# First v products from raw fp32 weights, a last product that accumulates in place, and a new order

## The chip, the cores and the metric

The kernel runs on one core of a Trainium2 chip. Its time is the device time of that core in microseconds (us). It is one program with five instruction queues: TensorE (PE in the rows), VectorE (DVE), ScalarE (ACT), GpSimd (POOL) and SyncE (SP), which only starts DMA transfers. Each queue runs in its own order, and the queues wait for each other by semaphores. The runs of the kernel before have a median of 493.95 us (492.88 to 494.36).

## The reference

One layer norm feeds two branches, and their product is added to the input:

```python
def _A_ref(x, wqkv, w_phi, wo):              # S = 2048 tokens, D = 512, H = 32 heads of 16
    q, k, v = (x @ wqkv) per head
    pq, pk  = q @ w_phi, k @ w_phi           # per head, 16 x 16
    phi_q   = concat(softmax(pq), softmax(-pq));  phi_k likewise
    kv, z   = phi_k^T v, sum over tokens of phi_k
    o       = (phi_q kv) / (phi_q z + 1e-6)
    return o @ wo
def _B_ref(x, w1, b1, w2):                   # F = 1792
    return mish(x @ w1 + b1) @ w2
xn  = layernorm(x)
out = x + _A_ref(xn, ...) * silu(_B_ref(xn, ...))
```

Everything is in fp32.

## The kernel before

**Number format.** Most matmuls take the fast fp32r format. An operand is split into a high part (a copy into fp32r on ScalarE) and a low part (source minus high part, on VectorE or GpSimd), by `split`, and a product of two split operands is three matmuls: low x high, high x low, high x high (`blocks`, `mm3`). Transposes, the folds of `w_phi` into the q and k weights, the kv sums and the numerators are plain fp32 matmuls.

**Seven products for eight.** The 2048 tokens are handled as 16 tiles of 128, two tiles to a chunk c. A chunk times a 512-row weight is computed as seven half-size products on sums and differences of the blocks. `norm(t)` normalizes and transposes tile t into the PSUM tile `pt`. For an even tile it splits the transposed blocks; for an odd tile it also forms the four differences `xs` and splits those (`fh`, `fl` hold the parts). For k and v these products are `kv_a` to `kv_d` (tiles `kx`, `ky`, `kz`). Chunk 0 is an exception: `FRONT = 1` sends it through `direct(c, i)` (tile `kj`), which takes the plain blocks, so that it needs no differences of the weights. i = 0, 1 give v of tiles 0 and 1, i = 2, 3 give k. Each `kj` is 12 matmuls of 128x512, since each of its four blocks takes three.

**Stages.** First the k weights are folded (`wkf`), then k and v of all chunks with the softmax features and their sums (`kvp`), mixed with the first FFN product of tokens 0 to 1023 (`fx`, `fy`, `fz`, parts Fa0 to Fd6). Then q (`qx`, `qy`, `qz`), the denominators (`den`), and the first FFN product of tokens 1024 to 2047 (Fa7 to Fd13). For these the split w1 blocks are loaded again from DRAM, tiles `w1b`, parts M0 to M6 (`again1`). Then numerators (`pn`), the output projection (`pw`), and the second FFN product (`y`, parts G), of which the last eighth of the tokens (T = 7) is done product by product over all seven weight blocks. `final` adds up its products, applies silu, multiplies and stores.

**What sets the order.** The code only records operations. `ORDER` lists the parts; TensorE runs its work in just that order. `Program.simulate` then places the other engines' operations around it: each has a due time (the TensorE time of what needs it, less its own duration, shifted by an entry of `SHIFT`), an operation recorded by `either` or `copy` may go to one of two engines, and tiles come from pools with a fixed number of buffers (38 of `slot`, 15 of `s2`, 8 PSUM banks). A tile is taken when its first operation is placed, and its buffer waits for the tile that held it before. What comes out is a fixed instruction list for each queue.

**Names in the rows.** Every operation is issued from one line, L397 before and L403 after. `wv0h`, `wv0l`, `wv1h`, `wv1l` are the parts of the raw v weights `wvr`; `wkh`, `wkl` those of the folded k weights; `ws1` to `ws4` the weight sums and differences. `xh`, `xl` (x12_) are the first half of tile 1. `xc` are the blocks of chunks 4 to 7. `hd` is the FFN's hidden layer in DRAM, `r` a block of it read back.

Of the kernel before, what the change touches and what calls it, by code (L numbers as in the profile page):

```python
# [39 lines left out]
A0 Kd2 Fa0 Ka4 Kb3 Fb0 Fc0 N10 Kc3 A1 Kb4 N11 Kd3 Fd0 A2 N14 N12 P4 Kc4 Ka5 Kd4 N13 Kb5 Kc5 Kd5 Fa4 Ka7 Fb4 Fc4 Ka6  # L40
N15 Fd4 Kb6 A3 P6 Kc6 Kb7 Kd6 Kc7 P2 A4 P3 A5 Fa6 Fa3 Fb6 Fa2 P1 Fb3 Fc6 Fc3 Kd7 P5 wQ Fa1 Fb2 Fd3 Fd6 M4 Fc2 A6 A7
Fa5 Fb1 Q0 Fb5 Fc1 z Fd1 Fc5 D0 D1 Q1 M3 Q2 D2 L D3 Q3 Fd5 Fa11 Fd2 Fa10 M5 Fa12 Fb10 Fb11 D4 Fc11 D5 Fc10 M6 Q4 Fd11
D8 D6 Q7 Fa13 wo0 D7 M1 Fb12 Fc12 Q5 D9 M0 Fd12 Fb13 wo1 D10 Fc13 Fa8 Fd10 D11 Q6 Fd13 Ub0 M2 Fb8 Fc8 Fd8 Fa9 Fa7 Fb7
Fb9 Ua0 Fc9 Fc7 O0 R0 D12 O5 D13 O7 O6 O1 D14 D15 Fd7 R2 O2 Ub1 Fd9 O3 R6 O4 Ua1 R1 G7 R3 G8 O9 O15 R4 O10 G9 O13 O11
G10 G11 O8 R5 O14 O12 G12 G13 G21 G35 G36 G37 E1 G38 H1 G22 G39 G40 G41 G23 G24 E5 G0 G25 G26 G27 G1 G2 G3 G28 E3 G29
H5 G30 G31 G32 G4 G5 G6 G33 G34 E4 E0 G42 G43 H4 G14 G15 G44 G45 G46 G16 G17 H3 H0 G18 G19 G47 G48 G20 E6 G49 E7 E2 H6
H2
# [2 lines left out]
N0:2:-4600 N0:5:5000 kh:3:-4800 N4:2:1800 N4:6:-2800 N1:15:300 N1:23:-3700 N1:24:4800 wq0:2:1600 wq0:4:900 N3:17:15000  # L50
ks:1:-500 ks:2:-4900 N5:14:-600 Kd0:7:-800 N7:10:-2000 N7:11:2000 N7:16:5800 Kb1:1:-5100 N8:1:5000 N8:11:2000
N9:5:3000 N9:6:-800 N9:7:-800 Kc1:2:3600 Fa0:3:7000 N10:1:300 N11:0:-5000 Kd2:3:-3000 Kd2:4:15000 Kd2:7:300 Kd3:3:2000
Ka5:3:5800 Kd4:3:-200 Kd4:9:2000 N15:13:-3600 Kd5:3:-2000 P6:1:-800 P6:10:1600 Fc4:4:-4200 P5:3:800 Kc6:9:-1100
Kc7:2:-800 Kc7:7:10000 Kc7:9:4700 Kd6:1:800 Kd6:3:-1700 A4:0:5800 Kd7:7:6800 Fc3:5:5000 Fa5:1:300 Fc2:1:-3000
wQ:2:-800 wQ:6:-5000 Q0:15:2000 Fc5:2:-5800 P1:12:-300 Fa1:4:-3200 Q2:13:1700 Q2:20:-600 Fb1:3:-2000 D3:0:1100
D3:1:300 Fc1:2:-7300 Q4:14:-3000 D5:6:1900 M5:3:2000 D6:4:-2500 D6:8:2300 M2:0:300 D8:10:-2000 D7:6:500 Q6:5:3900
Q6:16:8000 Q5:5:1700 Q5:20:-2000 Q5:25:5300 Fb12:3:800 D9:7:1300 Fd12:1:4200 Fd12:2:-5000 D11:6:4800 Ub0:4:-300
Ub0:12:-2800 Ub0:13:-1500 Fc9:2:5300 D13:0:7100 D13:1:-3400 D13:2:300 M1:2:11200 Q7:3:-6200 Q7:20:-4300 Q7:22:5000
Q7:23:-1300 Q7:25:4200 Fb7:1:1600 Ua0:11:5000 Ua0:14:2000 D14:1:700 D14:5:-5900 D14:7:600 Fc7:2:8300 D15:9:-2000
D15:10:-1300 R0:1:-1600 R0:5:800 Ub1:2:-2700 Ub1:12:10200 Fd8:1:1100 R2:7:-5000 R3:1:800 R1:7:5600 R5:4:300 R5:6:-5300  # L60
G10:1:5000 G11:2:800 R6:1:-5000 E1:0:-15000 O15:2:800 E4:0:-1300 E4:3:5000 G36:0:2000 G37:1:3800 G39:4:2500 G0:1:3200
G0:6:1200 G3:3:-5000 G3:5:12900 G22:0:2000 G5:6:1400 G23:6:700 G24:3:300 G27:1:300 H0:0:10000 G43:2:-3800 H5:3:2600
G14:5:-5000 G15:1:2000 G16:4:4800 G46:3:-2600 G47:6:-4100 H3:5:-5000 E2:2:-4700 E2:3:1300 G49:6:4200 G49:16:-1600
# [1154 lines left out]
```

## Time and profile before

| | |
|---|---|
| median of 3 runs | 493.95 us (492.88 to 494.36) |
| profiled execution | 493.94 us, of which the span of the core is 492.2 us |
| TensorE busy | 481.9 us, 98% of the span |
| VectorE busy | 455.8 us, 93% |
| ScalarE, GpSimd busy | 292.7 us (59%), 253.8 us (52%) |
| HBM | 60.60 MB read, 44.43 MB written |

The span is the profiler's time from the first to the last instruction of the core; 1.74 us of the execution lie outside it. In a row of the timeline the first number is the start, the second how long the group lasted, x8 that eight instructions were merged, and the bracket how long the engine had been idle and what ended that. PE rows are matmuls and PEld rows their weight loads, which overlap. One plain fp32 matmul is recorded as two instructions.

### The profile page before, as it was taken

What the parts mean: (1) busy time and instruction counts of PE and PEld (TensorE: products, weight loads), DVE (VectorE), ACT (ScalarE), POOL (GpSimd) and SP (SyncE); (2) the same over time, 40 slices, a digit from 0 to 9 for tenths busy, and PEclk for the clock granted to TensorE, in tenths of its full rate; (3) what the DMA queues carried; (4) which work ended last, traced back from release to release, by engine and by line L of the source; (5) the groups of instructions that cost most, each with busy time, mean ns of one, the idle gap of its engine ahead of it and who ended that gap; (6) DMA issues with size and microseconds to landing.
All of it is one profiled execution on the core that took longest, in us unless ns stands there. A gap on an engine that the chain in (4) does not pass through costs nothing.

```text
span 492.2 us, 10298 instructions
## 1 busy us (share of the span) xinstructions
PE 481.9 (98%) x3808; PEld 426.2 (87%) x3808; DVE 455.8 (93%) x897; ACT 292.7 (59%) x450; POOL 253.8 (52%) x196
## 2 busy tenths in 40 slices
PE   6999999999999999999999999999999999999996
PEld 6987878888888989889887778788899999999996
DVE  6999999999998889998999889989989999989984
ACT  2978556555555453633444535576778688598631
POOL 2689989988726356785757775470050302030010
PEclk8999999999999999999999999999999999999999
...
GB/s 291 226 107 55 200 237 83 281 159 294 317 368 366 306 207 243 388 367 249 118 157 326 233 90 298 99 225 192 173 193 164 202 192 161 207 192 278 153 136 56
DMA packets 68642, 105.70 MB, mean 215 GB/s; under 512 B 6896, under 2 KB 37744, under 8 KB 68592
## 3 DMA queue, kind: packets, MB, share of 16 engines
...
q10 hardware_dynamic: 144, 0.26, 0.1%
...
HBM read 60.60 MB, written 44.43 MB: 213 GB/s over the span
## 4 chain that ended last, share of the span: by engine, by line
PE 93%; DMA 4%; DVE 2%; SPq 1%; issue 0%; ACT 0%
PE y L397 29%; PE fx L397 15%; PE pw L397 9%; PE kx L397 8%; PE fy L397 8%; PE qx L397 4%; PE ky L397 4%; PE fz L397 3%; DMA w1b<-w1d 3%; PE kj L397 2%; PE qy L397 2%; PE kz L397 2%; PE pt L397 2%; PE pn L397 2%; PE kvp L397 2%; DMA wkT<-wqkT 1%
## 5 line engine op out<-in xcount | busy, mean ns | idle before, releaser
L397 ACT ACTIVATE ah<-r 128x896 fp32r<-128x896 f32 x56 | 51.2, 944 | 16.0 <-DVE r L397 11.0
L397 DVE TENSOR_TENSOR al<-r,ah 128x896 fp32r<-128x896 f32 x50 | 54.6, 1123 | 1.2 <-ACT ah L397 0.9
L397 POOL TENSOR_TENSOR r<-r 128x128 f32<-128x128 f32 (+1 forms) x18 | 9.2, 525 | 85.5 <-DVE r L397 35.1
L397 DVE TENSOR_TENSOR r<-r 128x128 f32<-128x128 f32 (+1 forms) x150 | 48.0, 367 | 2.6 <-ACT r L397 1.8
L397 PE MATMUL y<-w2h,al 128*128 128x256 f32 x160 | 45.4, 284 | 0.0
L397 PE MATMUL y<-w2l,ah 128*128 128x256 f32 x160 | 45.3, 283 | 0.0
L397 PE MATMUL y<-w2h,ah 128*128 128x256 f32 x160 | 45.3, 283 | 0.0
L397 PE MATMUL y<-w2t,ah 128*128 128x256 f32 x224 | 40.8, 283 | 0.0
L397 PE MATMUL fx<-fh,w1b 128*128 128x512 f32 x112 | 39.2, 394 | 0.9 <-DMA w1b<-w1d 0.9
L397 ACT ACTIVATE r<-r 128x512 f32<-128x512 f32 x56 | 33.4, 621 | 6.7 <-DMA r<-hd 6.7
L397 PEld LDWEIGHTS y<-w2t,ah 128*128 128x128 f32 x224 | 34.9, 192 | 0.0
L397 PE MATMUL y<-w2t,al 128*128 128x256 f32 x112 | 31.7, 283 | 0.0
L397 PEld LDWEIGHTS y<-w2h,al 128*128 128x128 f32 x160 | 30.7, 192 | 0.5 <-issue 0.4
L397 PEld LDWEIGHTS y<-w2l,ah 128*128 128x128 f32 x160 | 30.7, 192 | 0.1
L397 PEld LDWEIGHTS y<-w2h,ah 128*128 128x128 f32 x160 | 30.7, 192 | 0.0
L397 PE MATMUL y<-w2g,ah 128*128 128x256 f32 x160 | 30.4, 283 | 0.0
L397 PEld LDWEIGHTS fx<-fh,w1b 128*128 128x128 f32 x112 | 21.0, 188 | 6.7 <-DMA w1b<-w1d 1.7
L397 PEld LDWEIGHTS y<-w2g,ah 128*128 128x128 f32 x160 | 24.9, 192 | 0.0
L397 PE MATMUL fx<-fl,w1b 128*128 128x512 f32 x56 | 22.0, 392 | 0.9 <-DMA w1b<-w1d 0.9
L397 PE MATMUL y<-w2g,al 128*128 128x256 f32 x80 | 22.6, 283 | 0.0
L397 POOL TENSOR_TENSOR xx<-sr,xx 128x512 f32<-128x512 f32 x2 | 2.6, 1292 | 38.4 <-DVE xx L397 38.4
L397 PEld LDWEIGHTS y<-w2t,al 128*128 128x128 f32 x112 | 21.5, 192 | 0.0
...
## 6 DMA issues: line engine op xcount, KB each, us to landing
...
```

Of the source, the lines that this page charges most:

```text
L397: ins = getattr(e, m)(*a, **k)
```

## The change

1. For tiles 0 and 1, `norm` first copies the transposed tile from PSUM to an SBUF tile `xf` (`flat[t]`). All that read `pt` of these tiles read `xf` then. With the source in SBUF, GpSimd may do their low parts and differences as well (`tt = either`), and the copy `xr` of the first half is dropped for chunk 0.
2. v of tiles 0 and 1 (`direct`, i < 2) is computed as four plain fp32 matmuls of `xf` with the raw weights `wvr`, in place of twelve fp32r matmuls on split parts.
3. The masked copy `phit` of `w_phi` may run on GpSimd too.
4. In the last eighth of the FFN, the bank of product 2 is first filled with a copy of product 1, and product 2 accumulates on it. `final` then applies silu right out of PSUM and has no addition there.
5. `ORDER` and `SHIFT` are new tables, and one constant of the planner's transfer times changed.

```diff
 ORDER = """
-wv0 kh N0 N2 N6 kd N1 wv1 kl ks Ka0 wq1 b1 N3 wq0 Kd0 Kb0 N7 Ka1 Kc0 k2 k4 N4 N5 Kb1 N8 Kc1 Ka2 Ka3 N9 P0 Kb2 Kd1 Kc2
+wv0 N0 b1 N1 kh kl N2 N3 Kc0 wv1 Ka1 Kb0 kd N4 N6 ks wq0 N5 Kd0 Ka0 N7 Ka2 k2 wq1 Kb1 P0 k4 Kc1 Ka3 N8 N9 Kb2 Ka4 Kd1
...
@@ simulate
-                dma = max(dma, now + (1100 if now > 2500 else 1350) + (READ if reads(calls[0][1]) else WRITE))
+                dma = max(dma, now + (1100 if now > 2500 else 1750) + (READ if reads(calls[0][1]) else WRITE))
@@ block_kernel
-    V.tensor_tensor(phit.rearrange("p g (j b) -> p g j b", b=DH), phic[:, :, None, :].to_broadcast([P, KC, 8, DH]),
+    either(phit.rearrange("p g (j b) -> p g j b", b=DH), phic[:, :, None, :].to_broadcast([P, KC, 8, DH]),
@@ norm
+        if t < 2 * FRONT:
+            flat[t] = s2(f"xf{t}").rearrange("p (k n) -> p k n", k=KC)
+            copy(flat[t], pt)
+            pt = flat[t]
         c, p0 = t // 2, pts.get(t // 2)
+        tt = either if c < FRONT else V.tensor_tensor
...
-                    split(pt[:, 2 * x:2 * x + 2], *xc[c][x])
+                    split(pt[:, 2 * x:2 * x + 2], *xc[c][x], tt)
...
-        split(pt[:, 2:4], *xc[c][2])
-        x12 = alloc("s2", [P, 2, P], f"xr{c}")
+        split(pt[:, 2:4], *xc[c][2], tt)
...
-            split(pt[:, 0:2], *x12_[c])
-        copy(x12, pt[:, 0:2])
+            split(pt[:, 0:2], *x12_[c], tt)
+            x12 = pt[:, 0:2]
+        else:
+            x12 = alloc("s2", [P, 2, P], f"xr{c}")
+            copy(x12, pt[:, 0:2])
...
-            V.tensor_tensor(d[:, i], a, b, op=ALU.subtract)
+            tt(d[:, i], a, b, op=ALU.subtract)
@@ direct
-        lhs = [xc[c][0], xc[c][1]] if t % 2 == 0 else [x12_[c], xc[c][2]]
-        for j, (a, (h, l)) in enumerate(zip(((0, 1), ("k", 2))[i // 2], lhs)):
-            blocks(ps, lambda k: (h[:, k], l[:, k]), lambda k: tuple(t[:, k] for t in wkv[a]), j == 0, j == 1)
         if i < 2:
+            for j in range(2):
+                with one():
+                    for k in range(2):
+                        PE.matmul(ps, flat[t][:, 2 * j + k], wraw["v", j][:, k], start=j == k == 0, stop=j == k == 1)
             vs[t] = s2(f"v{t}")
...
+        lhs = [xc[c][0], xc[c][1]] if t % 2 == 0 else [x12_[c], xc[c][2]]
+        for j, (a, (h, l)) in enumerate(zip(("k", 2), lhs)):
+            blocks(ps, lambda k: (h[:, k], l[:, k]), lambda k: tuple(t[:, k] for t in wkv[a]), j == 0, j == 1)
@@ ffn2
-                            PE.matmul(ps, lhs[u], v, start=k not in opened, stop=b == NB - 1 and u == 0 and v is wh, skip_group_check=True)
+                            PE.matmul(ps, lhs[u], v, start=k not in opened and (n, last) != (2, True),
+                                      stop=b == NB - 1 and u == 0 and v is wh, skip_group_check=True)
...
+            if last and n == 2:
+                copy(at(2)[0], at(1)[0])
@@ final
-            if n == 8 and not DIRECT:
+            if n == 8:
                 u = base
-            else:
+            elif n != 2:
                 plus_(u, base, y(n))
-            A.activation(u, u, AF.Silu)
+            A.activation(u, y(2) if n == 2 else u, AF.Silu)
```

**What stands where: the start, on TensorE.** Before, behind the nine warm-up matmuls (wkf and wqf are folds, four matmuls each):

```order
L397 MATMUL wkf01_147<-phit_101,wkT00_137 128x128 x4
L397 MATMUL wkf11_148<-phit_101,wkT01_138 128x128 x4
L397 MATMUL pt0_154<-ident_83,x0_151 128x128 x4
L397 MATMUL pt2_162<-ident_83,x2_157 128x128 x4
L397 MATMUL pt6_170<-ident_83,x6_165 128x128 x4
L397 MATMUL pt1_178<-ident_83,x1_175 128x128 x4
L397 MATMUL wkf21_189<-phit_101,wkT10_139 128x128 x4
L397 MATMUL wkf31_190<-phit_101,wkT11_140 128x128 x4
L397 MATMUL kj00_194<-wv0h_142,fl00_104 128x512
```

In the change, at the same place:

```order
L403 MATMUL pt0_149<-ident_83,x0_146 128x128 x4
L403 MATMUL pt1_156<-ident_83,x1_153 128x128 x4
L403 MATMUL wkf01_164<-phit_101,wkT00_137 128x128 x4
L403 MATMUL wkf11_165<-phit_101,wkT01_138 128x128 x4
L403 MATMUL wkf21_169<-phit_101,wkT10_139 128x128 x4
L403 MATMUL wkf31_170<-phit_101,wkT11_140 128x128 x4
L403 MATMUL pt2_178<-ident_83,x2_173 128x128 x4
L403 MATMUL pt3_180<-ident_83,x3_175 128x128 x4
L403 MATMUL kj03_183<-wkh0_161,xl0_160 128x512
```

The transposes of tiles 0 and 1 now come first, and the first `kj` is k of tile 1, where it was v of tile 0. Behind the 12 matmuls of `kj03` and the products `kx1`, `kz1` of chunk 1 follow:

```order
L403 MATMUL kz1_193<-wv1h_190,fh10_105 128x512
L403 MATMUL kj01_195<-wvr0_141,xf1_157 128x512 x2
L403 MATMUL kj01_195<-wvr1_189,xf1_157 128x512 x2
L403 MATMUL pt4_206<-ident_83,x4_201 128x128 x4
L403 MATMUL pt6_214<-ident_83,x6_209 128x128 x4
L403 MATMUL wqf01_220<-phit_101,wqT00_218 128x128 x4
L403 MATMUL wqf11_221<-phit_101,wqT00_218 128x128 x4
L403 MATMUL pt5_223<-ident_83,x5_203 128x128 x4
```

The four `kj01` matmuls are the new fp32 ones.

**On ScalarE, at the same place** (from its first work on a matmul's result). Before:

```order
L397 ACTIVATE wkh0_144<-wkf01_147 128x512
L397 ACTIVATE x2_157<-x2_157,nb2_161,rs2_155 128x512
L397 ACTIVATE wv0h_142<-wvr0_141 128x1024
L397 ACTIVATE fh00_103<-pt0_154 128x2x128
L397 ACTIVATE wkh0_144<-wkf11_148 128x512
L397 ACTIVATE wv1h_184<-wvr1_183 128x1024
L397 ACTIVATE fh20_107<-pt1_178 128x2x128
L397 ACTIVATE fh00_103<-pt2_162 128x2x128
```

In the change:

```order
L403 ACTIVATE xf0_150<-pt0_149 128x512
L403 ACTIVATE fh00_103<-xf0_150 128x2x128
L403 ACTIVATE fh10_105<-xf0_150 128x2x128
L403 ACTIVATE xf1_157<-pt1_156 128x512
L403 ACTIVATE xh0_159<-xf1_157 128x256
L403 ACTIVATE fh20_107<-xf1_157 128x2x128
L403 ACTIVATE fh30_109<-xs0_158 128x2x128
L403 ACTIVATE wkh0_161<-wkf01_164 128x512
L403 ACTIVATE wv0h_142<-wvr0_141 128x1024
L403 ACTIVATE wkh0_161<-wkf11_165 128x512
L403 ACTIVATE fh40_111<-xs0_158 128x2x128
L403 ACTIVATE wkh1_166<-wkf21_169 128x512
```

Before, the high part of the first fold (`wkh0`) stood first; now seven activations on tiles 0 and 1 stand ahead of it. The next two after these rows are `wv1h` and the last `wkh1`.

**On SP, at the last loads of w1 for the first FFN product** (tiles w1b; hd are stores of the hidden layer). Before:

```order
L397 DMA w1b12_800<-w1d21_450 128x768 [waits DMAHW1_49,PE_49]
L397 DMA w1b02_799<-w1d20_449 128x768 [waits DMAHW2_49,PE_49]
L397 DMA hd36_768<-hb13_758 128x512 [waits DMAHW3_49]
L397 DMA hd26_719<-hd13_790 128x512 [waits DMAHW4_49,Activation_49]
L397 DMA hd31_806<-hc8_805 128x512 [waits DMAHW5_49,DVE_49]
L397 DMA w1b22_801<-w1d22_451 128x1024 [waits DMAHW6_49,Pool_49]
L397 DMA hd21_772<-hd8_807 128x512 [waits DMAHW7_49,Activation_49]
L397 DMA hd31_806<-hb8_804 128x512 [waits DMAHW0_49,DVE_49]
L397 DMA w1b32_802<-w1d23_452 128x1024 [waits DMAHW1_49,PE_49]
```

In the change:

```order
L403 DMA w1b12_781<-w1d21_382 128x768 [waits DMAHW3_49,PE_49]
L403 DMA w1b30_774<-w1d03_259 128x1024 [waits DMAHW4_49,PE_49]
L403 DMA hd23_656<-hd10_761 128x512 [waits DMAHW5_49,Activation_49]
L403 DMA hd35_760<-hb12_742 128x512 [waits DMAHW6_49,DVE_49]
L403 DMA w1b02_780<-w1d20_381 128x768 [waits DMAHW7_49,PE_49]
L403 DMA hd21_769<-ha8_768 128x512 [waits DMAHW0_49,DVE_49]
L403 DMA hd25_717<-hd12_770 128x512 [waits DMAHW1_49,DVE_49]
L403 DMA w1b22_782<-w1d22_383 128x1024 [waits DMAHW2_49,PE_49]
L403 DMA w1b32_783<-w1d23_384 128x1024 [waits DMAHW3_49,PE_49]
```

Which instruction each waits for stands in the program's wait counts. Before, the load of `w1b32` (the last block, fx9) waits for the second matmul of `fx7` on `fl01`, and 19 matmuls of 128x512 stand between that one and the first that uses `w1b32`; a little earlier, the load of `w1b21` (fx8) waits for a GpSimd scaling of tile 7's q features (`q7e`), which follows VectorE's denominators. In the change, between the matmul that each of the four loads of the last block waits for and its first use stand 120 to 148 matmuls; among the last sixteen loads the fewest behind such a wait are 54 (`w1b31`). Four of these sixteen wait for others: `w1b05`, `w1b11` and `w1b21` for GpSimd, `w1b25` for VectorE.

**The end, on VectorE.** Before:

```order
L397 TENSOR_TENSOR xx15_1_1182<-u15_1_1184,xx15_1_1182 128x256
L397 TENSOR_TENSOR u15_0_1187<-yc0_1171,y74_1170 128x256
L397 TENSOR_TENSOR u15_0_1187<-u15_0_1187,sr15_0_1186 128x256
L397 TENSOR_TENSOR xx15_0_1185<-u15_0_1187,xx15_0_1185 128x256
L1214 UNCONDITIONAL_BRANCH
```

In the change:

```order
L403 TENSOR_TENSOR u15_1_1195<-u15_1_1195,sr15_1_1194 128x256
L403 TENSOR_TENSOR xx15_1_1193<-u15_1_1195,xx15_1_1193 128x256
L403 TENSOR_TENSOR u15_0_1198<-u15_0_1198,sr15_0_1197 128x256
L403 TENSOR_TENSOR xx15_0_1196<-u15_0_1198,xx15_0_1196 128x256
L1234 UNCONDITIONAL_BRANCH
```

The addition of product 2 (`y74`) to product 1 is gone from the end of the queue. ScalarE's copy `y74<-y70` needs product 1 alone, and five products of 21 matmuls (6, 5, 7, 4 and 3) run on TensorE between product 1 and product 2.

More of the change, by code (lines that the diff above doesn't have):

```diff
@@ L38 @@
 ORDER = """
-wv0 kh N0 N2 N6 kd N1 wv1 kl ks Ka0 wq1 b1 N3 wq0 Kd0 Kb0 N7 Ka1 Kc0 k2 k4 N4 N5 Kb1 N8 Kc1 Ka2 Ka3 N9 P0 Kb2 Kd1 Kc2
[L40 to L47, printed above, removed]
+wv0 N0 b1 N1 kh kl N2 N3 Kc0 wv1 Ka1 Kb0 kd N4 N6 ks wq0 N5 Kd0 Ka0 N7 Ka2 k2 wq1 Kb1 P0 k4 Kc1 Ka3 N8 N9 Kb2 Ka4 Kd1
+Kc2 Kb3 A0 Fa0 Kc3 Kd2 Fb0 Fc0 P4 N10 A1 N11 Kd3 Fd0 Kb4 Kc4 N12 Fa4 Fb4 Kd4 P2 A2 Ka5 N13 Fc4 Fd4 N14 Kb5 Kc5 Ka6 N15
@@ new lines @@
+Kd5 Kb6 A3 A4 Fa2 Ka7 P6 Kc6 P3 Kb7 Kc7 Fb2 Kd6 Fa3 Fc2 Kd7 Fb3 Fa6 Fc3 Fb6 Fc6 P1 wQ Fa1 Fd6 Fb1 A5 A6 Fd3 A7 Fd2 M3
+P5 Q0 Fa5 Fc1 z Fb5 D0 Fc5 Q1 D1 Fd1 Q3 L D2 D3 Fd5 M4 Q2 M6 D4 Fa10 D5 Fb10 Fa11 Fb11 Fc10 Q4 Fc11 D6 Fa13 Fb13 Fc13
+Fd13 Q6 M5 Fa12 D8 Q5 D7 Fb12 D9 Q7 Fc12 Fd10 M1 Fa8 Fd12 M0 Fb8 Fd11 Fc8 M2 Fa7 D10 D11 Fd8 Ua0 Fb7 Fa9 Fb9 Ub0 wo1
+D12 Fc7 wo0 D13 Fc9 Fd9 O2 D14 D15 O4 Fd7 O6 O3 R2 O7 Ua1 R5 O1 Ub1 R0 O5 G7 R6 O0 O9 O11 O8 O13 O10 R3 R1 O14 G8 G9
+R4 G0 G10 G1 G11 G12 G13 G2 E1 G3 O15 O12 H1 G4 G21 G22 G23 G5 G24 G6 G25 G26 E0 G28 G27 G29 G30 H0 G31 G35 E3 G32 G36
@@ L48 @@
+H3 G37 G38 G39 G33 G34 G40 G41 E4 E5 G42 G43 G14 G44 G15 H4 H5 G45 G16 G17 G18 G46 G19 G47 G48 G20 E6 E2 H2 G49 H6 E7
 """
 SHIFT = """
[L50 to L63, printed above, removed]
@@ L64 @@
-G49:42:-300 G49:46:4700 E7:29:5000
+@:9:-1500 N0:2:300 N0:6:-300 kh:5:-300 kh:6:-15000 N4:3:-5000 N4:5:-2500 N4:9:-2800 N4:12:800 N1:0:300 N1:1:9800
+N1:16:-2000 N1:21:-14200 N1:22:-800 N2:1:-300 N2:8:-900 N2:14:-300 N3:15:3200 ks:0:-9900 N5:6:9300 N5:10:-6200
+N5:12:15000 Ka2:1:15000 k4:0:-2300 N6:0:6400 N6:14:3000 Kd0:4:4700 Kd0:6:300 Kd0:9:1100 Ka1:1:200 wq1:2:300 N8:4:-2200
+Kb2:1:-300 Kc1:1:800 Kc1:3:11400 Kd1:5:-4200 Kd1:6:300 Kc2:7:500 Fa0:1:-800 N11:1:-8800 N11:8:-800 Kc3:5:3700
+Fc0:5:5000 Kd2:4:3500 Kd3:1:3100 Kd3:4:2600 Ka5:1:2300 Ka5:3:2000 A3:0:-5000 P4:3:-1600 N15:4:-2000 N15:9:7800
@@ new lines @@
+Kc5:1:2800 Kd5:9:4000 P6:5:-800 P6:10:5600 N13:7:-4200 Fb4:3:-800 Kb6:3:800 P5:0:8900 P5:4:-1700 Kc6:1:-7200 Kd6:4:300
+P2:1:-300 P2:7:-5800 P2:10:-7500 Fd6:1:2300 A7:1:14700 Q0:11:500 Q0:21:-4600 Q0:23:-7300 z:0:-4000 z:4:-2000 z:6:-6900
+z:12:500 P1:4:-2000 P1:9:6300 D0:4:3800 D1:6:-1700 Fd2:1:-8900 Q2:20:300 Q1:16:-4300 M6:0:-5000 Q3:16:-3600 L:10:-1900
+Fa11:3:-5000 D3:3:10000 D3:5:800 D3:7:500 Fc13:4:2000 Q4:3:-2000 Q4:5:-5000 Q4:9:-900 Q4:23:-1400 D5:6:1300 Fb10:1:800
+Fd11:1:-10000 D6:6:-1100 M2:1:-2300 D7:5:-1100 Fa12:1:300 Fa12:4:-10200 Q6:9:500 Q6:24:12800 Q5:5:-9800 Q5:7:5000
@@ new lines @@
+Q5:20:-3800 Fb12:3:1500 D9:1:-2000 D9:4:2800 Fc12:2:500 D10:2:15000 D10:3:5000 D11:6:-2800 Ub0:11:2000 Ub0:13:300
+Ub0:14:1100 D12:0:-800 D12:1:-500 wo1:1:-1100 wo1:2:-800 M0:0:800 M0:3:2700 D13:2:-6000 D13:8:-10700 D13:9:-300
+Q7:16:300 Ua0:9:300 Ua0:14:300 D14:0:-4700 D14:10:5700 D15:0:4500 D15:4:-4500 D15:5:-5700 Fc8:2:12800 O2:2:-7800
+R0:2:300 Ub1:2:-800 O4:2:300 R2:10:300 R3:1:4800 G8:2:-3200 Ua1:8:-2000 Ua1:12:-2800 Ua1:16:13000 G10:2:800 O11:2:800
+G28:1:800 G28:6:-9300 R4:3:5000 R4:7:-5000 G11:2:3100 G11:3:1900 G11:4:-1700 R6:8:-3600 G32:3:-800 G32:5:-800
@@ new lines @@
+G35:0:300 E1:2:7300 G34:4:5900 G37:4:300 G38:0:-4100 G39:0:-800 G39:2:2500 G39:3:-300 G39:6:4400 G40:0:300
+G40:1:-10000 G0:3:-5000 G0:4:-5600 G1:1:-5000 H4:2:6700 G3:6:-3200 G41:6:1300 E5:6:-300 G22:3:-300 G22:6:1200
+G25:2:7300 G25:3:-9100 G26:5:-800 G42:3:2000 E0:1:4400 G27:0:4400 H1:4:2000 H1:9:-3000 E3:3:5300 E3:6:6900 G43:2:-6400
+G44:0:-5000 G44:6:300 G14:0:10500 G14:5:4200 G17:6:-5000 G46:4:-1400 G18:0:6600 G18:2:-300 G18:5:4700 G19:2:300
+G19:6:-600 G47:4:2000 H3:4:-800 G48:2:-5800 G48:5:800 E6:1:300 E2:1:-800 E2:4:12900 G49:16:1100 G49:22:5500
@@ L65 @@
+G49:34:-300 G49:47:3000 H6:3:-10000 H2:0:7000 H2:5:-5000 E7:1:-5000 E7:4:3900 E7:12:-300 E7:20:-800 E7:24:-300
+E7:26:4200 E7:27:-200
 """
@@ L570, in block_kernel @@
     xd = dram.tile([P, 2, 7, 2, 4, P], F32, name="xd")
-    xc, x12_, pts, tiles, fx = {}, {}, {}, {}, {}
+    xc, x12_, pts, tiles, fx, flat = {}, {}, {}, {}, {}, {}
     def blocks_x(q):
```

## The prediction

> **What bounds the kernel now.** First the page: the shares of the engines, and the chain that ended last.
>
> ```profile
> PE 481.9 (98%) x3808; PEld 426.2 (87%) x3808; DVE 455.8 (93%) x897; ACT 292.7 (59%) x450; POOL 253.8 (52%) x196
> PE 93%; DMA 4%; DVE 2%; SPq 1%; issue 0%; ACT 0%
> ```
>
> TensorE is busy for all but 10.3 us of 492.2. Busy is not the same as at full pace, so I then read who it waited for, and the chain piece by piece (start, length, work):
>
> ```profile
> PE wkf L397 <- DVE mv L397: 2.3, 1, 2.3
> PE fx L397 <- DMA w1b<-w1d: 1.7, 2, 0.9
> PE wake L397 <- DVE mhalf L520: 1.1, 1, 1.1
> PE wkf L397 <- DMA wkT<-wqkT: 0.7, 1, 0.7
> ```
>
> ```profile
> 9.47 2.08 PE wkf L397 x8
> 11.54 2.53 PE pt L397 x16
> 14.08 1.79 PE wkf L397 x16
> 15.86 2.76 PE kj L397 x12
> 18.62 1.78 PE wqf L397 x16
> ...
> 267.31 1.42 PE fx L397 x5
> ...
> 283.23 1.65 PE fx L397 x6
> ...
> 359.29 128.52 PE y L397 x1071
> ```
>
> These waits are 5.8 us, and TensorE's last product ends at 359.29 + 128.52 = 487.81, which leaves a tail of 4.4 us: together 10.2, all of the idle time. Between 9.47 us and the tail it loses 1.7 us by waits, all at two loads of w1. So the time is TensorE's work, plus the start, plus these two stalls, plus the tail. VectorE, at 93%, is what a wait would come from. In this form I cost the change: it alters all four terms.
>
> **The fp32 products.** Two `kj` groups of 12 fp32r matmuls go, 2 x 2.76 = 5.5 us. Eight fp32 matmuls of 128x512 come. The trace has none of that width. The nearest is the fold: 16 records are eight fp32 matmuls of 128x128 in 1.78 us, so 0.22 each, and four times the columns make 0.89; eight are 7.1. That is +1.6 us, on TensorE's path in full. Bounds: if each took two passes at the fp32r pace (2.76 / 12 = 0.23), eight would take 3.7, or -1.8; at the pace of the folds at 9.47 (2.08 for four, 0.52 each), 16.6, or +11, which needs a slow clock after 20 us, and the rows show none there. I take +1.6, by the fold at full pace.
>
> **The start.** The groups up to the first `kj` are the same in both: four folds, four transposes, one `kj`; before, they end at 15.86 + 2.76 = 18.6. Now they begin with tile 0, and behind it stands ScalarE. The rows with the durations:
>
> ```profile
> 3.90 0.69 DVE L397 BATCH_NORM_STATS2 st<-x 128x6 f32<-128x512 f32 x1 [2.58 <-DMA x<-x]
> 4.63 0.18 DVE L397 BATCH_NORM_AGGREGATE mv<-st 128x2 f32<-128x6 f32 x1
> 7.20 0.12 DVE L397 TENSOR_SCALAR rs<-mv 128x1 f32<-128x1 f32 x1
> 7.40 0.56 POOL L397 TENSOR_TENSOR rs<-rs,mhalf 128x1 f32<-128x1 f32 x1 [5.47 <-DVE rs L397]
> 9.49 0.18 DVE L397 TENSOR_SCALAR nb<-mv,rs 128x1 f32<-128x1 f32 x1
> 10.47 0.81 ACT L397 ACTIVATE x<-x,nb,rs 128x512 f32<-128x512 f32 x1 [1.10 <-DVE nb L397]
> 11.20 1.04 ACT L397 ACTIVATE wv0h<-wvr 128x1024 fp32r<-128x1024 f32 x1
> 12.44 0.39 ACT L397 ACTIVATE fh<-pt 128x256 fp32r<-128x256 f32 x1 [0.20 <-PE pt L397]
> 15.15 0.59 ACT L397 ACTIVATE wkh<-wkf 128x512 fp32r<-128x512 f32 x1
> 16.01 0.68 DVE L397 TENSOR_TENSOR wkl<-wkf,wkh 128x512 fp32r<-128x512 f32 x1
> 18.72 0.60 ACT L397 ACTIVATE v<-kj 128x512 f32<-128x512 f32 x1
> ```
>
> Tile 0 is in at 3.90. Statistics, power, shift and scale add 0.69 + 0.18 + 0.12 + 0.56 + 0.18 + 0.81 = 2.5, with steps of about 0.1 between engines 6.9; four transposes (2.53 for sixteen) 0.6. From 7.6 on ScalarE has 14 activations in a row up to the last `wkh`: two copies `xf` (0.60), six splits of 256 columns (0.39), four `wkh` (0.59), two `wvh` (1.04), 8.0 us, so until 15.6. One low part (0.68) and the last two matmuls of the group later it is 17.2. The start gains 18.6 - 17.2 = 1.4 us; bounds: nothing, if the transfers of the weights end the row of activations later, and 2.3, if the activations up to the splits find TensorE's clock and the banks ready.
>
> Then comes what the old order didn't have. PSUM has eight banks; here two `pt`, four `wkf`, `kj03` and `kx1` fill them. So `kz1` waits until VectorE has read the first fold's bank for the weight differences, six VectorE operations behind the last `wkl` (some 1.8 us at 0.2 to 0.6 each), which is 0.4 us after `kx1` (1.4 us) ends. Two groups later `wqf11` and `pt5` wait for VectorE's softmax of `kj03` and its copy of `wqf01`: from 16.4, 28 VectorE operations end near 28, TensorE is there at 26.5, 1.2 us lost. `wqf31` waits for the copy of `wqf21` just before it, an activation of 0.60 with its steps: 0.9. Sum +2.5. That is argued from the queues, with nothing like it in the rows: after 9.47 the old order waits for no VectorE operation in the start. Bounds: 0, if VectorE runs ahead (the change takes the masked copy and some splits off it), and +4.5, if each of these waits doubles. I take +2.5, net of the start +1.1.
>
> **The two stalls at w1.** The view of the tile `w1b` gives the time from issue to landing of its 28 loads:
>
> ```profile
> DMA to landing us min/median/max: 3.0/5.9/8.5
> ```
>
> and the timeline the second half of the first stall:
>
> ```profile
> 267.31 0.50 PE L397 MATMUL fx<-fl,w1b 128*128 128x512 f32 x1 [0.85 <-DMA w1b<-w1d]
> ```
>
> The stall at 283 is a load that becomes free 19 matmuls before it is used (4.3 us at 0.23), less than the median 5.9 us. The one at 267 waits for a load that the denominators hold up by way of GpSimd. In the change the matmul waits leave 54 to 148 matmuls, 12 us or more, and only four of the last sixteen loads wait for GpSimd or VectorE. So both stalls go: -1.7 by the waits, and the first group after each restarts slowly (1.42 for five and 1.65 for six, against 1.15 and 1.38 at 0.23), another 0.55: -2.25. Bounds: 0, if new loads come late in their place, and -2.25. What is late next there: nothing that the order shows, since by the order the output weights start to load some 14 us of matmuls ahead of their first use.
>
> **The tail.** The rows behind the last product:
>
> ```profile
> 487.84 0.42 DVE L397 TENSOR_TENSOR u<-yc,y 128x256 f32<-128x256 f32 x1 [0.66 <-PE y L397]
> 488.29 0.42 ACT L397 ACTIVATE u<-u 128x256 f32<-128x256 f32 x1 [2.04 <-DVE u L397]
> 488.74 0.42 DVE L397 TENSOR_TENSOR u<-u,sr 128x256 f32<-128x256 f32 x1 [0.48 <-ACT u L397]
> 489.20 0.43 DVE L397 TENSOR_TENSOR xx<-u,xx 128x256 f32<-128x256 f32 x1
> ```
>
> The addition and its step, 488.29 - 487.84 = 0.45, go; silu reads PSUM instead. The copy of product 1 lies beside five products of 21 matmuls (12.6 us at 128.52 / 1071 = 0.12), so it costs nothing; without that cover it would be an activation of 0.4. -0.45, bounds 0 and -0.5.
>
> **Nothing for the rest.** The two `xf` copies are counted in ScalarE's row. The masked copy on GpSimd lies ahead of the power of tile 0 (bound: its power 0.5 later). The moves after chunk 1 lie under TensorE's unbroken work; VectorE, the only cover that is thin, has 875 operations in the new list and 883 in the old.
>
> **Sum.** +1.6 + 1.1 - 2.25 - 0.45 = 0.0 on 493.94 us, the profiled execution, which stands at the median of the runs (493.95). Forecast 493.9.
>
> **Rivals.** *The order simply works* (faster): VectorE runs ahead, no bank is late, so only -1.4 at the start: +1.6 - 1.4 - 2.25 - 0.45 = -2.5, 491.4. The windows (their length, then the busy time of PE, PEld and DVE) speak on both sides:
>
> ```profile
> 0.00:12.00 12.00, 7.87 (x38) 7.41 (x39) 7.81 (x28) 3.40 (x4) 3.59 (x13) 0.89 0.82 288
> 12.00:25.00 13.00, 13.00 (x89) 11.88 (x88) 12.95 (x33) 12.32 (x26) 7.83 (x5) 0.97 0.68 223
> ```
>
> VectorE is idle for 12.00 - 7.81 = 4.2 us ahead of 12 us and could do part of its work there; from 12 to 25 it has no idle time.
>
> *TensorE starts cold* (slower): its clock sank behind the start, in which TensorE was idle for 12.00 - 7.87 = 4.1 us:
>
> ```profile
> 8.00:10.00 2.00, 1.27 (x9) 1.08 (x8) 1.87 (x8) 0.60 (x1) 0.70 (x1) 0.83 1.01 381
> 10.00:12.00 2.00, 2.00 (x12) 2.00 (x11) 2.00 (x8) 1.52 (x2) 1.21 (x2) 0.50 1.02 388
> 12.00:14.00 2.00, 2.00 (x15) 1.85 (x14) 2.00 (x5) 1.80 (x4) 0.00 (x0) 0.81 1.05 406
> ```
>
> (Column seven is the granted clock.) With it the folds and transposes from 9.47 took 2.08 and 2.53, against 0.89 and 1.74 at the later pace: 2.0 us. In the change TensorE has gaps until ScalarE's row ends near 16, and then would run its first dense 4 us slowly: +2.0 on top of the bank waits, and with one w1 stall left (1.2): +1.6 + 1.1 + 2.0 - 1.05 - 0.45 = +3.2, 497.1. It decides if the clock is below 0.9 after 17 us. The Trainium skill's page "TensorE: Matmul & The Clock Gate", section "Part 1: The HAM clock gate", speaks for this rival: the array is at half clock by default and after an idle window of about 3.4 us, and full speed needs about as long a busy stretch. The trace agrees in kind, with 0.50 at 10 to 12 us.
>
> *The fp32 products are cheap* (two passes, -1.8 instead of +1.6): 493.9 - 3.4 = 490.5; nothing in the folds speaks for it.
>
> **How the numbers follow.** A measurement of this kernel can tell about 0.3% (1.5 us) from no change. Forecast 0.42 (its own range 492.4 to 495.4), the order works 0.32, cheap fp32 0.06, cold 0.20. So faster 0.38, same 0.42, slower 0.20. The range reaches from 490.3 to 497.5, just past the outer two of them; what their own spread puts beyond is left out.
>
> **What would show it.** In the changed profile: `kj` on `xf` at 0.9 us a matmul; the first 12-matmul `kj` ending near 17.2; TensorE waits on VectorE or ScalarE between 18 and 42 us of about 2.5 us in all; no wait for `w1b`; 0.45 less behind the last product. I am wrong if the waits on PSUM banks are absent (then it is faster) or the clock is low after 17 us, or if a new wait stands in the middle, where I see none.

## The result, and the profile after

The changed kernel takes 500.06 us (median of 4 runs, 499.00 to 501.62), the kernel before 493.41 (492.77 to 494.36): a ratio of 1.0122, 95% interval 1.0093 to 1.0152. It is slower by 1.2%, outside the range of the forecast. The profiled execution took 500.88 us, of which 498.9 are the span, 6.7 more than before. The page's shares, and the answer to the question for whom TensorE waited (total, times, longest):

```profile
PE 486.0 (97%) x3800; PEld 426.8 (86%) x3800; DVE 450.6 (90%) x895; ACT 291.9 (59%) x453; POOL 258.7 (52%) x194
```

```profile
PE fy L403 <- ACT hc L403: 2.2, 1, 2.2
PE pt L403 <- ACT x L403: 1.9, 2, 1.4
PE pn L403 <- issue: 1.3, 1, 1.3
PE y L403 <- DVE yy L403: 0.9, 1, 0.9
PE wqf L403 <- ACT wqf L403: 0.8, 1, 0.8
```

No wait for `w1b` is left: both stalls at w1 are gone. Three waits are new: `fy` for ScalarE's `hc`, `pn` (the numerators) for nothing that a semaphore shows, `y` for VectorE's `yy`. They stand at 73, 292 and 442 us, in the middle and late part of the kernel, where the forecast saw none.

To add up the difference I took, for every matmul, the distance to the next one's start, and subtracted the usual distance for its kind (0.227 us for 512 columns, 0.120 for `y`, 0.429 for each of the two records of an fp32 product of 512). What is left over is lost time, whether the engine was idle or the clock slow. By stage, in us of the profiled executions (the times of the second column are those of the changed kernel):

| stage | us | lost before | lost after | difference |
|---|---|---|---|---|
| start, to the first products of k and v | 0 to 18 | 10.4 | 9.2 | -1.3 |
| first chunks, folds of q | 18 to 42 | 0.7 | 2.7 | +2.0 |
| | 42 to 73 | 0.7 | 0.2 | -0.5 |
| k features and first FFN product | 73 to 80 | 0.3 | 4.1 | +3.8 |
| | 80 to 260 | 2.3 | 2.5 | +0.2 |
| stalls at w1; numerators | 260 to 300 | 3.0 | 2.5 | -0.5 |
| | 300 to 330 | 0.4 | 0.7 | +0.3 |
| second FFN product | 330 to the last matmul | 0.0 | 1.6 | +1.6 |
| behind the last matmul | | 4.6 | 4.1 | -0.5 |
| TensorE's own work | | 469.8 | 471.2 | +1.4 |
| sum, before rounding | | 492.2 | 498.9 | +6.7 |

**The start ended when it was forecast to.** TensorE's timeline in the changed kernel (start, length):

```profile
17.17 0.39 PE L403 MATMUL kx<-wv0h,fl 128*128 128x512 f32 x1
20.35 3.59 PE L403 MATMUL kj<-wvr,xf 128*128 128x512 f32 x8
23.78 1.04 PE L403 MATMUL pt<-ident,x 128*128 128x128 f32 x8
39.18 1.16 PE L403 MATMUL wqf<-phit,wqT 128*128 128x128 f32 x8 [0.77 <-ACT wqf L403]
```

The first `kj` group ends where `kx` starts, at 17.2. A group of four fp32 products lasts from 20.35 to 23.78, 3.43 us, so one is 0.86.

**The wait at 73 us.** TensorE, ScalarE and GpSimd there, and the windows behind it (the seventh column is the granted clock):

```profile
70.82 2.41 POOL L403 TENSOR_TENSOR zacc<-zacc,k3e 128x1024 f32<-128x1024 f32 x1
73.17 1.07 POOL L403 TENSOR_TENSOR k7e<-k7p,k7m 128x512 f32<-128x512 f32 x1
74.19 1.07 POOL L403 TENSOR_TENSOR k7e<-k7m,k7p 128x512 f32<-128x512 f32 x1
75.29 0.69 ACT L403 ACTIVATE hc<-fy,b1t 128x512 f32<-128x512 f32 x1 [3.50 <-POOL k7e L403]
73.40 0.39 PE L403 MATMUL fx<-fh,w1sh 128*128 128x512 f32 x1
76.03 0.50 PE L403 MATMUL fy<-fh,w1sl 128*128 128x512 f32 x1 [2.25 <-ACT hc L403]
77.27 0.63 PE L403 MATMUL fy<-fl,w1sh 128*128 128x512 f32 x1
```

```profile
76.00:78.00 2.00, 1.97 (x6) 1.55 (x7) 1.95 (x5) 0.93 (x1) 0.00 (x0) 0.70 0.22 88
78.00:80.00 2.00, 2.00 (x41) 1.54 (x43) 1.65 (x3) 0.60 (x1) 1.86 (x3) 0.50 0.16 61
80.00:82.00 2.00, 2.00 (x48) 1.78 (x41) 1.48 (x4) 0.67 (x2) 1.86 (x3) 0.95 0.32 121
```

`fy` needs a PSUM bank that `hc` reads. `hc` itself reads nothing that GpSimd makes; what it can wait for is a buffer that `k7e` still reads (`hc` and `k7p`, which `k7e` reads, come from the same pool). And `k7e` stands behind a sum (`zacc`) of 2.4 us. The wait costs 2.63 - 0.23 = 2.4 us from start to start; after it the clock falls to 0.5, and the next products take 0.43 us apart (76.84, 77.27, 77.69 are their starts) in place of 0.23. With them it comes to 3.8.

**The gap in the numerators.** `pn` is a group of 64 small fp32 matmuls, recorded as 128. Here are the group before it, which runs through, and the one with the gap:

```profile
278.20 2.75 PE L403 MATMUL pn<-ph,kvw 32*32 32x256 f32 x128
289.27 2.84 PE L403 MATMUL pn<-ph,kvw 32*32 32x256 f32 x110
293.44 0.68 PE L403 MATMUL pn<-ph,kvw 32*32 32x256 f32 x18 [1.33 <-issue]
```

The next product starts 2.69 us after the first of these groups and 4.78 us after the second (294.05), so the gap costs 2.1 us.

**The wait at 442 us.** VectorE and TensorE:

```profile
439.33 2.22 DVE L403 TENSOR_TENSOR al<-r,ah 128x896 fp32r<-128x896 f32 x2 [0.36 <-POOL al L403]
441.47 0.41 DVE L403 TENSOR_TENSOR yc<-yy,y 128x256 f32<-128x256 f32 x1
441.94 0.38 PE L403 MATMUL y<-w2m,al 128*128 128x256 f32 x1
443.42 0.35 PE L403 MATMUL y<-w2h,al 128*128 128x256 f32 x1 [0.86 <-DVE yy L403]
```

Two low parts (`al`) of 1.1 us each stand on VectorE ahead of the additions that free the banks.

**The tail** lost its addition, as forecast:

```profile
494.99 0.38 ACT L403 ACTIVATE u<-y 128x256 f32<-128x256 f32 x1 [1.58 <-PE y L403]
495.41 0.43 DVE L403 TENSOR_TENSOR u<-u,sr 128x256 f32<-128x256 f32 x1 [1.08 <-ACT u L403]
495.87 0.43 DVE L403 TENSOR_TENSOR xx<-u,xx 128x256 f32<-128x256 f32 x1
```

### The profile page after: what moved, and what is told of

Read it like the earlier page. It is cut to its first block, busy times and chain, and to the rows that moved or that the text cites. A ratio compares the mean times of both kernels' runs of the same rounds, so it can differ in the third digit from the quotient of the medians.

```text
span 498.9 us, 10311 instructions
## 1 busy us (share of the span) xinstructions
PE 486.0 (97%) x3800; PEld 426.8 (86%) x3800; DVE 450.6 (90%) x895; ACT 291.9 (59%) x453; POOL 258.7 (52%) x194
## 5 line engine op out<-in xcount | busy, mean ns | idle before, releaser
L403 DVE TENSOR_TENSOR al<-r,ah 128x896 fp32r<-128x896 f32 x51 | 57.5, 1146 | 4.4 <-ACT ah L403 2.9
L403 DVE TENSOR_TENSOR r<-r 128x128 f32<-128x128 f32 (+1 forms) x153 | 46.2, 343 | 5.9 <-ACT r L403 5.2
L403 POOL TENSOR_TENSOR xx<-sr,xx 128x512 f32<-128x512 f32 x1 | 1.3, 1297 | 42.2 <-DVE xx L403 42.2
L403 POOL TENSOR_TENSOR al<-r,ah 128x896 fp32r<-128x896 f32 x5 | 10.7, 2140 | 22.2 <-DVE r L403 19.8
```

Source lines behind the costliest of these rows:

```text
L403: ins = getattr(e, m)(*a, **k)
```

## The experiments

The theory after the result: each of the three new waits is a local matter of one queue's order, and they are the whole loss. The first rival: the engines behind are full, so a wait that is removed comes up again. The second question was which part of the change brought the waits, the edits or the tables. All ratios are to the kernel before, with 95% intervals.

| run | median us | ratio |
|---|---|---|
| the change | 500.06 | 1.0122 (1.0093 to 1.0152) |
| e1_pool | 497.66 | 1.0073 (1.0043 to 1.0103) |
| e2_phase | 498.89 | 1.0130 (1.0076 to 1.0184) |
| e3_vec | 500.99 | 1.0129 (1.0086 to 1.0171) |
| e4_all | 497.77 | 1.0089 (1.0055 to 1.0124) |
| e5_banks | 498.92 | 1.0107 (1.0075 to 1.0139) |
| e6_both | 495.97 | 1.0044 (1.0025 to 1.0063) |
| e7_oldorder | 516.35 | 1.0464 (1.0431 to 1.0497) |
| e8_tail | 493.32 | 1.0001 (0.9984 to 1.0017) |
| e9_const | 517.97 | 1.0488 (1.0430 to 1.0546) |
| e10_phit | 518.62 | 1.0501 (1.0475 to 1.0527) |
| e11_splitv | 508.47 | 1.0295 (1.0275 to 1.0314) |
| e12_const2 | 501.70 | 1.0149 (1.0120 to 1.0179) |

For e1 and e3 to e6 the finished plan was taken, and single operations were moved in one engine's row before it was issued; every other row stayed as it was, but for two of SyncE's loads in e3 (below). (The buffers and banks that tiles get can still change with such a move, since a tile takes what is free.) e2 adds matmuls to TensorE's row, and e4 has all three edits. e9 and e10 have two executions each, the others four to ten.

**e1_pool: GpSimd's sum behind `k7e`.**

```diff
 # GpSimd's row
-zacc<-zacc,k3e
 k7e<-k7p,k7m
 k7e<-k7m,k7p
+zacc<-zacc,k3e
```

> GpSimd's sum of the k features of tile 3 (zacc<-zacc,k3e, 2.4 us) is put behind the two k7e operations; nothing else moves. Theory (the wait at 73 us is a buffer: hc takes the buffer that the second k7e has to free, and the sum of 2.4 us stands ahead of it): k7e ends some 2.4 us earlier, hc starts as soon as its matmuls are done, TensorE's wait of 2.2 us falls below 0.4, and the slow matmuls behind it (0.43 for 0.23 us each, 1.2 us in all) go too. About -3.5 us: 496.5. Rival (VectorE and GpSimd are full there, so the wait only comes up again some us later): less than 1 us gained, 499.2 or more.

The rows at that place:

```profile
71.42 1.06 POOL L403 TENSOR_TENSOR k7e<-k7m,k7p 128x512 f32<-128x512 f32 x1
72.44 2.41 POOL L403 TENSOR_TENSOR zacc<-zacc,k3e 128x1024 f32<-128x1024 f32 x1
72.51 0.69 ACT L403 ACTIVATE hc<-fy,b1t 128x512 f32<-128x512 f32 x1 [1.14 <-POOL k7e L403]
73.25 0.50 PE L403 MATMUL fy<-fh,w1sl 128*128 128x512 f32 x1
```

`hc` follows `k7e` at once, and `fy` runs on with no wait of its own listed. The lost time of that stage falls from 4.1 to 0.4 us: that the wait hangs on the sum ahead of `k7e` is shown. In time it gave 500.06 - 497.66 = 2.4 us, where 3.5 were expected (the two intervals overlap). Two things can make it less. `y` waits 2.1 us in this execution (1.2 for `yc`, 0.9 for `yy`), but that needn't come from the edit: with the same row of VectorE it waits 1.6 us in e2 and 2.8 in e12. And the slow clock behind the wait isn't paid each time. In e5 (below), which has the same wait of 2.2 us at the same place, the clock stays at 1.00:

```profile
76.00:78.00 2.00, 2.00 (x18) 1.53 (x22) 1.97 (x6) 0.77 (x2) 0.10 (x1) 1.00 0.32 125
78.00:80.00 2.00, 2.00 (x71) 1.82 (x68) 2.00 (x3) 0.98 (x3) 2.00 (x4) 1.00 0.36 136
```

So 2.4 of the 3.8 us are the wait, and 1.4 a clock that fell in the profiled executions of the change, e2, e3 and e12 and not in that of e5.

**e2_phase: 32 more records ahead in TensorE's row.**

```diff
+    for _ in range(8):
+        nc.tensor.matmul(wake[:, 0:64], ones, ones[:, 0:64], start=True, stop=True)
     for _ in range(WAKE):
```

> Eight fp32 matmuls of 128x64 stand ahead of the warm-up matmuls, 32 more records in TensorE's row; every queue is otherwise the same. Theory (the gap of 1.7 us inside the numerators at 292 us, which no semaphore explains, is TensorE's code: a block of 16 KB starts to load at 291.08 and TensorE is at its end): 32 records earlier is 3.6 us earlier at the pace of the fx matmuls, so the gap and the slow restart go: about -2.0 us, 498.0. Rival (the load is late because of the transfers around it, whatever the place of the block's end): the gap stays or stands at other numerators, 500.0. The eight matmuls cost at most 1 us in the start, beside the wait of 1.4 us for tile 0.

The numerators now:

```profile
290.45 2.36 PE L403 MATMUL pn<-ph,kvw 32*32 32x256 f32 x94
294.27 1.05 PE L403 MATMUL pn<-ph,kvw 32*32 32x256 f32 x34 [1.47 <-issue]
```

In the window behind them the granted clock is 0.53 (in the change it is 1.00 there):

```profile
296.00:298.00 2.00, 2.00 (x6) 1.58 (x6) 2.00 (x6) 1.57 (x5) 2.00 (x2) 0.53 0.82 251
```

The gap didn't go. It moved: it stood behind 110 of the 128 records, and now stands behind 94. That is 16 matmul records, with their weight loads 32, just what was put ahead. In the runs on the plan of the change the gap is always behind 110 (the change itself, e1, e3, e5, e6, e12) or, with the eight matmuls, behind 94 (here and in e4), although the group starts at times up to 5 us apart. So it hangs on the place in TensorE's code and on nothing in the data. The median fell by 1.2 us, but the ratio to the kernel before didn't (1.0130 for 1.0122). What was wrong is the size: I took the block's load to be asked for so early that 32 records of the slow `fx` part would cover it. A load starts inside the group here too: the gap's end follows the start of TensorE's code load (291.08 in the change, 291.61 here) by 2.4 and 2.7 us, and the group's 256 records, weight loads included, last about 2.7 us undisturbed. How far ahead the load is asked for is not settled, and a shift large enough to take the block's end out of the group was not tried. The profile's table of transfer queues (packets, MB, share) has the loads:

```profile
q8 instruction: 30, 0.49, 0.4%
```

30 loads of 16 KB for some 7,600 records of matmuls and weight loads, one for each 256. The Trainium skill's page "Runtime: NRT & Kernel Launch", section "Instruction fetch mechanics", says that code is refilled in 16 KiB blocks of 256 instructions and that crossing into a new block is mostly hidden. The size of the blocks agrees with the row above; that the crossing is hidden doesn't hold for this group.

A block's end inside a group isn't enough to stop it, though. Counted over TensorE's matmuls, weight loads and waits in the traces, the gap stands within one record of the 4,289th in all nine runs on the new tables, and a second, smaller one (0.59 us, in e1's and e6's last group) stands 768 records, three blocks, behind it. In steps of 256, a block ends inside each of the four `pn` groups of the change. Two of them lose nothing, the second 2.1 us, the last 0.3. By the same count one ends inside the second group of the kernel before too, and that group runs through in 2.68 us. What differs is the load: there one starts at 279.06, 7 us ahead of the group, while in the change none starts between 278.64 and 291.08. Why it comes so late is open.

**e3_vec: the low parts behind the additions.**

```diff
 # VectorE's row
-al2_0<-r2_0,ah2_0
-al2_3<-r2_3,ah2_3
 yc5, yy5, yy4, yy5, yy4, yy5   (six additions that read the banks)
+al2_0<-r2_0,ah2_0
+al2_3<-r2_3,ah2_3
```

> On VectorE the low parts al2_0 and al2_3 (1.1 us each) are put behind six additions that read the PSUM banks of the second FFN product; nothing else moves. Theory (the wait at 442 us is those two operations ahead of the additions that free the banks): the wait of 0.9 us and the two small ones go: about -1.3 us, 498.8. Rival (VectorE is the bound of that stretch: al2_0 is then late by as much): 0 to -0.3 us, 499.9.

Nothing was gained: the additions now wait themselves, the first for ScalarE's copy `yy`, and that stands behind an `ah` that waits for GpSimd:

```profile
440.78 0.95 ACT L403 ACTIVATE ah<-r 128x896 fp32r<-128x896 f32 x1 [1.32 <-POOL al L403]
441.64 0.37 ACT L403 ACTIVATE yy<-y 128x256 f32<-128x256 f32 x1
442.04 0.42 DVE L403 TENSOR_TENSOR yc<-yy,y 128x256 f32<-128x256 f32 x1 [1.61 <-ACT yy L403]
```

The theory was too simple: which addition comes first matters, not only what stands ahead of it. It isn't a clean test either, since one of SyncE's loads of `r` moved with it, from 444.5 to 438.0 us.

**e4_all: e1, e2 and e3 together.** The three edits above in one kernel.

> The three edits together: GpSimd's sum behind k7e, eight small matmuls ahead, the two low parts behind the additions. If the three gaps are separate and nothing takes their place, -3.5 -2.0 -1.3 = -6.8 us: 493.3, no different from the kernel before. Rival (the new order has another limit behind them, such as VectorE's rate, which then shows): 496 or more.

497.77, no better than e1 alone. The rival's number is the nearer one. The wait at 73 us is gone, the gap in the numerators is 1.7 us, and the eight matmuls cost the start some 0.6 us (9.7 lost up to 18 us, for 9.2).

**e5_banks: the additions that free two banks first.**

```diff
 # VectorE's row
 yy4<-yy4,y41
+yy4<-yy4,y42
+yy4<-yy4,y43
 al2_0<-r2_0,ah2_0
 al2_3<-r2_3,ah2_3
 yc5<-yy5,y50
```

> In the changed kernel, VectorE's two additions that free the banks y42 and y43 are put ahead of the low parts al2_0 and al2_3; nothing else moves. Theory (the wait at 442 us is a question of which bank comes free first; the run that put the low parts behind all additions failed because yc5 has to wait for ScalarE's copy): y63 and y62 then take the banks of y42 and y43, free near 440 us, and their waits (0.2, 0.9 us) go; y20, 26 matmuls later, may wait some 0.3 us for yc5. About -1.0 us: 499.0. Rival (VectorE is simply behind by 1 to 2 us in this stretch): the wait moves to y20, total unchanged, 500.

No wait of `y` is left in the answer on TensorE's waits; the others stand:

```profile
PE fy L403 <- ACT hc L403: 2.2, 1, 2.2
PE pt L403 <- ACT x L403: 1.7, 1, 1.7
PE wake L403 <- DVE mhalf L538: 1.1, 1, 1.1
PE pn L403 <- issue: 1.1, 1, 1.1
PE wqf L403 <- ACT wqf L403: 0.8, 1, 0.8
```

The lost time from 330 us on falls from 1.6 to 0.0, and the median by 1.1 us (the intervals overlap, so the traces carry this, not the time). The wait varies between executions: with VectorE's old order, in the change, e1, e2 and e12, `y` waits 0.9 to 2.8 us around 442 us; with the new one, here and in e6, not at all. `y42` and `y43` are complete by about 435 us, where VectorE reads them here without a wait; in the change it simply reads them last.

**e6_both: e1 and e5.**

> The changed kernel with GpSimd's sum behind k7e and the two bank-freeing additions ahead. If both waits go: -3.7 and -1.0, 495.4. If VectorE is behind as soon as TensorE comes 3.7 us earlier to the second FFN product (as the run with GpSimd's sum alone showed: y waits of 2.8 us for 1.6), 497.

495.97, 4.1 us less than the change, between the two numbers. The trace tells what is left: no loss at 73 us, none at 442, but a new wait where the next banks change hands, since VectorE has seven low parts in a row ahead of `yc` there:

```profile
473.47 0.39 PE L403 MATMUL y<-w2h,al 128*128 128x256 f32 x1 [1.40 <-DVE yc L403]
```

With what is lost there (1.9 us from 330 us on) and the gap in the numerators (2.1 us), some 4 us stay lost that the kernel before doesn't lose, against 2.2 us of difference in time.

**e7_oldorder: all edits, with the old tables and the old constant.** One index of the old `SHIFT` was moved by one, for the addition that is gone.

```diff
-wv0 N0 b1 N1 kh kl N2 N3 Kc0 ...
+wv0 kh N0 N2 N6 kd N1 wv1 kl ...
-(1100 if now > 2500 else 1750)
+(1100 if now > 2500 else 1350)
```

> All edits of the change, with the tables and the planner's constant of the kernel before. Theory (the edits cost what the forecast said and the new tables bring the waits): fp32 products +1.4 (two groups of 3.43 us for two of 2.73), tail -0.5, both stalls at w1 stay, start within 1 us: 493.4 + 0.9 = 494.3, to 495.3. Rival (the edits themselves bring waits, by the copies xf in ScalarE's row or by another choice of engines): 496 or more.

516.35, 23 us over the kernel before. The waits:

```profile
PE pt L397 <- ACT x L397: 8.4, 3, 7.0
PE pn L397 <- DVE ph L397: 3.2, 1, 3.2
PE wkf L397 <- DMA wkT<-wqkT: 3.1, 1, 3.1
PE kvp L397 <- DVE k14e L397: 2.2, 1, 2.2
```

The theory that the edits are cheap and the new tables bring the waits falls in this form. But the waits are spread over the whole kernel, the largest near 74 us, far behind the edits. So the next pair of runs changed the plan without changing the work.

**e9_const and e10_phit: the kernel before with a nudge to its planner.**

```diff
 # e9_const
-(1100 if now > 2500 else 1350)
+(1100 if now > 2500 else 1750)
 # e10_phit
-V.tensor_tensor(phit..., phic..., bmask..., op=ALU.mult)
+either(phit..., phic..., bmask..., op=ALU.mult)
```

> The kernel before with only the planner's constant changed (transfer time at the start 1750 for 1350); no work is added or taken away, TensorE's row is the same, but the planner then places hundreds of operations of the other engines otherwise. Theory (a table of due times fits one plan only, and any edit that moves the plan brings waits, which is why the edits under the old tables took 516): 497 or more. Rival (the 22 us of that run come from the edits' own work, the copies and the fp32 products): 493 to 495.

> The kernel before with only the masked copy phit free to run on GpSimd as well; one operation of 0.6 us, the rest of the work is the same. By the same two theories: 497 or more if any move of the plan under the old tables brings waits; 493 to 495 if the 22 us came from the copies and the products.

517.97 and 518.62: one number in the planner, with not one operation more or less, costs 24 us. The largest waits of e9 are those of e7:

```profile
PE pt L397 <- ACT x L397: 9.8, 3, 8.8
PE pn L397 <- DVE ph L397: 3.2, 1, 3.2
PE kvp L397 <- DVE k14e L397: 2.0, 1, 2.0
PE wkf L397 <- DMA wkT<-wqkT: 1.5, 1, 1.5
```

So the old `SHIFT` fits one plan closely. Each of the three runs that moved that plan at its start, e7, e9 and e10, is 22.5 to 25 us slower, and so e7's 516 says nothing of what the edits themselves cost.

**e8_tail: the kernel before, with the last product's accumulation alone.** It stands at the end of the plan, and so only a handful of rows of three engines move.

```diff
+            if last and n == 2:
+                copy(at(2)[0], at(1)[0])
...
-            else:
+            elif n != 2:
                 plus_(u, base, y(n))
-            A.activation(u, u, AF.Silu)
+            A.activation(u, y(2) if n == 2 else u, AF.Silu)
```

> The kernel before with one edit: the last product accumulates on a copy of product 1, and silu reads PSUM. Forecast's term: -0.45 us by the span of the rows behind the last matmul, which 3 rounds can hardly tell in the time: 493.0. Rival (the copy or the reading of PSUM costs as much as the addition): rows behind the last matmul as long as before, 4.4 us.

493.32 for 493.81, ratio 1.0001 (0.9984 to 1.0017): not to be told from no change. The rows behind the last matmul do shorten, from 4.6 to 4.2 us counted from the same point, as the forecast's term has it. So the rival, that the copy or the reading of PSUM costs as much as the addition, is out.

**e11_splitv and e12_const2: nudges to the changed kernel.**

```diff
 # e11_splitv: v of tiles 0 and 1 by fp32r products again
-PE.matmul(ps, flat[t][:, 2 * j + k], wraw["v", j][:, k], ...)
+blocks(ps, lambda k: (h[:, k], l[:, k]), lambda k: tuple(t[:, k] for t in wkv[j]), j == 0, j == 1)
 # e12_const2
-(1100 if now > 2500 else 1750)
+(1100 if now > 2500 else 1350)
```

> The changed kernel with v of tiles 0 and 1 again by twelve fp32r matmuls each, everything else as in the change. By the products' own price -1.4 us, 498.7, if the plan holds. If the new tables fit only the plan with the fp32 products, the plan moves and new waits come: 503 or more.

> The changed kernel with the planner's constant of before (1350 for 1750): here only some ten operations of the first 15 us move (the copy xf of tile 1 goes to VectorE, a low part of tile 0 to GpSimd). Theory: few moves, small difference, 499 to 501, and the three waits at 73, 292 and 442 us stand as in the change. Rival: the start alone gains or loses over 1.5 us.

Undoing the fp32 products under the new tables makes the kernel slower, 508.47, though TensorE's own work falls by 1.4 us: these tables too depend on the plan. Ahead of the numerators TensorE's row has 16 records more and three waits fewer than in the change, and the gap stands behind 103 records for 110: again the same place in the code. The constant alone moved some ten operations here and cost nothing that the intervals can tell: 501.70, with the same three waits as the change, the one at 442 us longer (2.8 us in all).

## Why the prediction was wrong, step by step

- **The fp32 products**, +1.6: right. 3.43 us for a group of four, for 2.73 of the twelve, is +1.4 for the two; the fold's price of 0.89 stood against 0.86 measured. The rival of the cheap product is out.
- **The start**, -1.4: right in size, and partly by luck. The first `kj` group ends at 17.17, forecast 17.2, and the stage up to 18 us loses 1.3 less. ScalarE's row ends at 15.63, forecast 15.6, but it isn't what TensorE waits for: TensorE runs unbroken from 8.34, with its folds at a clock of 0.63 and 0.51 up to 12 us, and comes to the last low part's matmul at 16.72, 0.4 us after that part is done. My sum as told (15.6, a low part of 0.68, two matmuls of 0.23) makes 16.7, not 17.2. In e2 and e4 `kj` does wait for VectorE's low part, 0.23 us.
- **The waits on banks and VectorE behind it**, +2.5: right in kind and nearly in size. From 18 to 42 us it is +2.0, and 0.5 comes back up to 73. Of the single ones, `wqf31`'s wait for ScalarE's copy was put at 0.9 and measured 0.77; `kz1` lost 0.35 for the 0.4; `wqf11` and `pt5` lost 0.31 and 0.20 for the 1.2 that I gave them, and what ended `pt5`'s wait was ScalarE's `fh`, not VectorE's copy.
- **The stalls at w1**, -2.25: right. No load of `w1b` is waited for any more, and by the distances of the matmuls the two had cost 2.4 us in the kernel before.
- **The tail**, -0.45: right, -0.49. By the time alone it can't be told from nothing (e8).
- **"The moves after chunk 1 lie under TensorE's unbroken work"**: this failed. I took TensorE's unbroken work in the old profile as a cover that the new plan inherits. It was not a cover; it was the outcome of a plan in which each buffer and bank came free in time. The new plan has three places where TensorE has to wait: 3.8 us at 73 us with the slow clock behind it, 2.1 in the numerators, 1.6 at the second FFN product, 7.5 together. (In the numerators it was TensorE's code that came late, not a buffer.) I had weighed VectorE by the number of its operations (875 and 883, where the profiles have 895 and 897), and GpSimd for this stretch not at all; the largest of the three hung on GpSimd's row, by way of a buffer.
- **The sum.** The five terms that I had measured together about +1.4 + 0.3 - 2.4 - 0.5 = -1.2, a little better than the 0.0 forecast. The three waits that I hadn't make +7.5, and the rest is small gaps. The range ended at 497.5 and allowed one mishap of 3 us, by a cold start.
- **The rivals.** The cold start didn't come: the clock is low where it was before, from 8 to 12 us, and 1.00 from 12 us on. A slow clock came at another place, behind the wait at 73 us. "The order simply works" is out too.

What is shown: the wait at 73 us is GpSimd's sum ahead of `k7e` (e1), that at 442 us the order of VectorE's additions (e5, e6), and the gap in the numerators hangs on TensorE's place in its code (e2, e4, e11). By the time alone only e6, with both moves, is clear of the change. What is argued only: that the 4 us left in e6 would bring the change level with the kernel before. What stays open is why the planner put these operations so, when TensorE's code is asked for, and when a wait costs clock. None of the runs beats the kernel before.
